# Two batches of a decode attention kernel taken pair by pair: one score loop, one pV loop, both softmaxes between them, the FFN first

## The chip, the cores and the metric

The kernel runs on one core of a Trainium2 chip. The metric is the device time of one execution in microseconds (us). Before the change it was 351.21 us, the median of five runs (350.96 to 351.4). The profiled executions have a span that is about 2 us shorter than the time of the run (349.2 us against 350.98), because the span starts and ends with the recorded instructions.

## The reference, cut to what matters

```python
# x: [2, 1, 512]   k_cache, v_cache: [2, 32, 4096, 128] bf16   wq: [512, 4096]   wo: [4096, 512]
q = (x @ wq)                       # 32 heads of 128, one query for each of 2 batches
p = softmax(q . k * 128 ** -0.5)   # over 4096 keys, for each head and batch
a = (p . v) @ wo
b = relu(x @ w1) @ w2              # FFN, 512 -> 1376 -> 512
g = sigmoid((x * gate_w).sum(-1))
return g * a + (1 - g) * b
```

K and V are 67 MB each, the weights 11 MB. All of it is read once: 145.43 MB.

## The kernel before

The heads are taken two at a time: a "pair" is two heads of one batch, 2 MB of K and 2 MB of V, and there are 32 pairs. One queue, that of SyncE, issues all large loads in one fixed order. Four buffers (`NSLOT`) hold pairs of K first and pairs of V afterwards. A load waits until the buffer's last user is done, so at most four pairs are in flight or in use:

```python
load("ld_wq", wq_sb[:, :, :], wq_in)
for n in range(64):                  # 0..31: K pairs, 32..63: V pairs
    waits = []
    if n >= NSLOT:
        prev = n - NSLOT             # the buffer is free after the last transpose of K pair prev,
        waits.append(f"T_{prev}_7" if prev < 32 else f"pv_{prev - 32}")   # or the last pV of V pair prev
    load(f"ld_kv_{n}", kv_sb[:, n % NSLOT, :, :], kv_in(n), waits=waits, sem=f"slot{n % NSLOT}")
    if n == 12:
        load("ld_w1", ...); load("ld_w2a", ...); load("ld_w2b", ...)
# ... then wo in five parts
```

For a K pair, TensorE transposes 64 blocks of 128x128 (`T`), VectorE and ScalarE copy them out of PSUM, and 16 matmuls make scores (`Sc`). For a V pair, 64 matmuls with two columns each accumulate pV (`PV`). TensorE's work is in loops of four pairs. Batch 0 has pairs 0 to 15, and its softmax runs while the scores of batch 1 are made. The softmax of batch 1 runs while pV of batch 0 is made:

```python
for g in range(2):                   # two score loops on TensorE
    P.begin_loop(NIT) ... T(g, p, ...), Sc(g, p) ... P.end_loop()
# ...
for i in range(32):
    evac(i)                          # copies out of PSUM (VectorE, ScalarE)
    if i == 17: row_max(0)           # softmax of batch 0, inside the K stage
    if i == 18: exps(0)
    if i == 19: denom_l(0)
ptrans(0)                            # transposes of the exponentials
denom(0)
# ...
for i in range(PER):
    stage_p(i)                       # exponentials of pair i, laid out for pV (VectorE)
    if i == 1:
        row_max(1); exps(1); denom_l(1)
for g in range(2):
    if g:
        ptrans(1); ...stage_p...; denom(1)
        ffn_h(); ffn_relu(); ffn_f() # FFN between the two pV loops
    P.begin_loop(NIT) ... PV(g, p) ... P.end_loop()
    ...
o_spread()
proj()                               # times wo, added to the FFN in PSUM
```

Of the kernel before, what the change touches and what calls it, by code (L numbers as in the profile page):

```python
# [14 lines left out]
PER = 4  # L15
NPAIR = 16
NIT = NPAIR // PER
NKT = 2
# [118 lines left out]
def bass_gated_mix__gqa_block_cached__dense_activation_relu__decode_kernel(  # L137
# [49 lines left out]
    oA = sb("oA", [128, 2, 32, 4], b16)  # L187
    os_sb = sb("os_sb", [128, 32, 2], b16)
    out_sb = sb("out_sb", [98, 128], b16)

# [39 lines left out]
    def kv_in(n):  # L230
        c = A_k_cache if n < 32 else A_v_cache
        b, hp = divmod(n % 32, 16)
        return c[b, 2 * hp:2 * hp + 2].rearrange("h (p r) d -> (h p) r d", p=64)
# [6 lines left out]
    load("ld_gw", gw_sb[:, :], gw_in, eng="act")  # L240
    load("ld_wq", wq_sb[:, :, :], wq_in)
    for n in range(64):
        waits = []
        if n >= NSLOT:
            prev = n - NSLOT
            waits.append(f"T_{prev}_7" if prev < 32 else f"pv_{prev - 32}")
        load(f"ld_kv_{n}", kv_sb[:, n % NSLOT, :, :], kv_in(n), waits=waits, sem=f"slot{n % NSLOT}")
        if n == 12:
            load("ld_w1", w1_sb[:, :, :], w1_in)
            load("ld_w2a", w2_sb[:, 0:10, :], w2a_in)  # L250
            load("ld_w2b", w2_sb[0:96, 10, :], w2b_in)
    WO_CUTS = (0, 16, 24, 28, 30, 32)
# [60 lines left out]

    def T(g, p, qs):
        for q in qs:
            for rr in range(8):
                r = 8 * q + rr

                def waits(t, q=q):
                    i = NPAIR * g + PER * t + p  # L320
                    w = [f"ld_kv_{i}"] if q == 0 else []
                    if q >= 4:
                        w.append(f"ev_{i}_{q - 4}")
                    elif p:
                        w.append(f"ev_{i - 1}_{q + 4}")
                    return w + (["qm_0", "qm_1", "g"] if g == 0 and p == 0 and q == 0 else [])

                P.add("pe", lambda e, iv, q=q, rr=rr, r=r: e.transpose(bank16(4 + q % 4, rr * 128, 128), kv_sb[:, p, r, :], ident16[:, :]),  # L328
                      waits=waits if rr == 0 else [],
                      signal=(lambda t, q=q: f"T_{NPAIR * g + PER * t + p}_{q}") if rr == 7 else None)  # L330

    def Sc(g, p):
        for c in range(8):
            for hh in range(2):
                def waits(t, c=c):
                    i = NPAIR * g + PER * t + p
                    return ([f"qst_{i}"] if c == 0 else []) + ([f"ev_{i}_{c}"] if c >= 4 else [])

                P.add("pe", lambda e, iv, c=c, hh=hh: e.matmul(  # L339
                    S_chunk(g, c), lhsT=qst[:, p, hh, :], rhs=kt_sb[:, p % NKT, 8 * c:8 * c + 8, 64 * hh:64 * hh + 64],  # L340
                    start=False, stop=True, tile_position=(0, 32 * (c % 4)), skip_group_check=True),
                    waits=waits if hh == 0 else [],
                    signal=(lambda t: f"sc_{NPAIR * g + PER * t + p}") if (c, hh) == (7, 1) else None)

# [12 lines left out]
    def stage_q(i):  # L357
        p = i % PER
        P.add("pool", lambda e: e.tensor_copy(out=qst[:, p, :, :], in_=qmask[:, 2 * i:2 * i + 2, :]),  # L359
              waits=[f"qm_{i // NPAIR}"] + ([f"sc_{i - PER}"] if i >= PER else []), signal=f"qst_{i}", sem=f"qs{p}")  # L360

    for g in range(2):
        P.begin_loop(NIT)
        T(g, 0, range(8))
        for p in range(PER):
            if p + 1 < PER:
                T(g, p + 1, range(2))
            Sc(g, p)
            if p + 1 < PER:
                T(g, p + 1, range(2, 8))  # L370
        P.end_loop()


    def row_max(g):
        P.add("dve", lambda e: e.tensor_reduce(out=m4[:, g:g + 1], in_=S_region(g), axis=AX.X, op=ALU.max),  # L375
              waits=[f"sc_{NPAIR * g + NPAIR - 1}"], signal=f"m4_{g}")
        for q in range(4):
# [38 lines left out]
    def stage_p(i):  # L416
        g, hp = divmod(i, NPAIR)
        p = i % PER
        for hh in range(2):
            base = PSB[0:64, 2048 * g:2048 * g + 2048].rearrange("p (b k j) -> p b k j", b=2, k=32)  # L420
            P.add("dve", lambda e, hh=hh, base=base: e.tensor_copy(  # L421
                out=pst[64 * hh:64 * hh + 64, p, :, hh].rearrange("p (b k) -> p b k", b=2), in_=base[:, :, :, 2 * hp + hh]),
                waits=[f"pt_{g}_2", f"pt_{g}_3", "c_ps"] + ([f"pv_{i - PER}"] if i >= PER else []),
                signal=f"pst_{i}" if hh else None, sem=f"ps{p}")

    def o_norm(i):
        g, hp = divmod(i, NPAIR)
        P.add("dve", lambda e: e.tensor_tensor(out=oT[:, g, 2 * hp:2 * hp + 2], in0=o_col(i % PER), in1=rg[:, g, 2 * hp:2 * hp + 2],  # L428
                                               op=ALU.mult),
              waits=[f"pv_{i}", f"rg_{g}"], signal=f"oT_{i}", sem=f"on{i % PER}")  # L430

    def PV(g, p):
        for r in range(64):
            b, blk = p_place(r)

            def waits(t):
                i = NPAIR * g + PER * t + p
                return [f"ld_kv_{32 + i}", f"pst_{i}"] + ([f"oT_{i - 2}"] if i >= 2 else [])
            P.add("pe", lambda e, iv, r=r, k=32 * b + blk: e.matmul(o_col(p), lhsT=kv_sb[:, p, r, :], rhs=pst[:, p, k, :],  # L439
                                                                    start=(r == 0), stop=(r == 63)),  # L440
                  waits=waits if r == 0 else [], signal=(lambda t: f"pv_{NPAIR * g + PER * t + p}") if r == 63 else None)


    def ffn_h():
        for ft in range(11):
            n = 128 if ft < 10 else 96
            for t in range(4):
                P.add("pe", lambda e, ft=ft, t=t, n=n: e.matmul(  # L448
                    bank(MISC, 64 + 2 * ft, 2, 0, n), lhsT=w1_sb[:, t, ft:1280:10] if ft < 10 else w1_sb[:, t, 1280:1376],
                    rhs=xT_sb[:, t, :], start=(t == 0), stop=(t == 3)),  # L450
                    waits=["ld_w1", "rg_1"] if ft + t == 0 else [], signal="hT" if (ft, t) == (10, 3) else None)

    def ffn_relu():
        P.add("act", lambda e: e.activation(out=hr_sb[:, 0:20], in_=bank(MISC, 64, 20), func=ACT.Relu), waits=["hT"])  # L454
        P.add("act", lambda e: e.activation(out=hr_sb[0:96, 20:22], in_=bank(MISC, 84, 2, 0, 96), func=ACT.Relu), signal="hr")
        for n, lo, hi in ((128, 0, 10), (96, 10, 11)):
# [4 lines left out]

    def ffn_f():
        for ft in range(11):
            n = 128 if ft < 10 else 96
            for c in range(4):
                P.add("pe", lambda e, ft=ft, n=n, c=c: e.matmul(
                    acc(c), lhsT=hT_sb[0:n, ft, :], rhs=w2_sb[0:n, ft, 128 * c:128 * c + 128], start=False, stop=True,
                    tile_position=(0, 32 * c), skip_group_check=True),
                    waits=["hTs", "ld_w2a", "ld_w2b"] if ft + c == 0 else [])

# [13 lines left out]
    def proj():  # L484
        for r in range(32):
            for c in range(4):
                w = (["os_sb"] if r == 0 else []) + ([f"ld_wo_{WO_CUTS.index(r)}"] if r in WO_CUTS else [])
                P.add("pe", lambda e, r=r, c=c: e.matmul(acc(c), lhsT=os_sb[:, r, :], rhs=wo_sb[:, r, 128 * c:128 * c + 128],  # L488
                                                         start=False, stop=True, tile_position=(0, 32 * c), skip_group_check=True),
                      waits=w if c == 0 else [], signal="proj" if (r, c) == (31, 3) else None)  # L490

    for i in range(32):
        stage_q(i)
    for i in range(32):
        evac(i)
        if i == 17:
            row_max(0)
        if i == 18:
            exps(0)
        if i == 19:  # L500
            denom_l(0)
    ptrans(0)
    denom(0)
    P.add("pe", lambda e: e.matmul(bank(ACC, 0, 128), lhsT=zt[:, 0:128], rhs=zt[:, 0:128], start=True, stop=True))
    for i in range(PER):
        stage_p(i)
        if i == 1:
            row_max(1)
            exps(1)
            denom_l(1)  # L510
    for g in range(2):
        if g:
            ptrans(1)
            for i in range(PER):
                stage_p(NPAIR + i)
            denom(1)
            ffn_h()
            ffn_relu()
            ffn_f()
        P.begin_loop(NIT)  # L520
        for p in range(PER):
            PV(g, p)
        P.end_loop()
        for i in range(NPAIR * g, NPAIR * g + NPAIR):
            o_norm(i)
            if i + PER < NPAIR * (g + 1):
                stage_p(i + PER)
    o_spread()
    proj()
    P.add("dve", lambda e: e.tensor_copy(out=out_sb[:, :], in_=bank(ACC, 0, 128, 0, 98)), waits=["proj"], signal="res")  # L530
    for b, eng in enumerate(("sp", "act")):
# [53 lines left out]
```

## Time and profile before

| | value | where it is read |
|---|---|---|
| time | 351.21 us | median of five runs |
| bytes read, share of the 16 DMA engines | 145.43 MB, 98.3% | table of DMA queues |
| a 2 MB pair on the wire | 4.89 us | step between landings |
| TensorE for a K pair, unhindered | 4.80 us | timeline |
| TensorE for a V pair | 1.86 us | timeline |
| last score to first pV | 3.3 us | chain of waits |
| instruction fetches (queue q8; e8, with longer TensorE code, has 22 where e2 has 10) | 13 of 16 KB | table of DMA queues |

These lines of the page of the kernel before are the busy shares of the span in 40 slices (each digit a tenth) and the DMA queues. A queue's columns are packets, MB, and the share of sixteen engines' time.

```profile
span 349.2 us, 11060 instructions
...
PE   2489999995699899999998643343266643443244
...
PEclk9999999999599999999999555555555555555555
DMA  8999999999999999999999999999999999999994
GB/s 331 419 426 428 428 430 423 430 423 411 428 425 428 423 428 430 424 432 428 428 426 430 423 424 432 424 428 432 428 426 432 418 426 430 430 430 426 426 420 158
...
q1 hardware_dynamic: 10488, 145.43, 98.3%
q8 instruction: 13, 0.21, 0.3%
```

The DMA row is 9 from the second slice to the last but one. TensorE is also at 9 in the K stage, but only because it works at the pace of the loads (4.80 us of work a pair, and a pair lands every 4.89 us), and in the V stage (from slice 23 on) it waits most of the time (1.86 us of work in 4.89). The kernel is bound by the bytes: the loads take 98.3% of the sixteen engines' time. No change to an engine's work can save time here unless it also changes what the DMA queue does (e4 fills a hole in TensorE's work and stays at 350.96 us against 351.04).

The chain of waits of the kernel before, at the boundary between the K and the V stage (start us, duration us, what; L339 makes scores, L400 transposes the exponentials, L409 sums denominators, L439 is pV):

```profile
185.89 1.54 PE PS L339 x16
187.43 1.82 PE PS L400 x64
189.25 0.35 PE PS L409 x2
...
190.77 3.19 PE PS L439 x116
193.96 3.07 issue
```

From the last score at 187.43 to the first pV at 190.77 there are 3.3 us. Pair 0 is finished at about 192.5, estimated from the 3.19 us of 116 matmuls, and then the load of V pair 4 is requested.

The stages of 2 us of the same kernel around that time (window, PE busy (count), PEld, DVE, ACT, POOL, granted TensorE clock, DMA share, GB/s):

```profile
194.00:196.00 2.00, 0.00 (x0) 0.00 (x0) 0.82 (x5) 1.09 (x2) 0.00 (x0) 0.50 1.02 414
196.00:198.00 2.00, 0.96 (x36) 0.97 (x37) 1.17 (x7) 0.00 (x0) 0.00 (x0) 0.50 0.98 418
198.00:200.00 2.00, 2.00 (x81) 2.00 (x79) 0.62 (x4) 0.00 (x0) 0.00 (x0) 0.50 1.04 442
200.00:202.00 2.00, 0.58 (x22) 0.50 (x19) 0.00 (x0) 0.00 (x0) 0.00 (x0) 0.50 0.99 410
```

The DMA share stays at 1: V pair 4 was requested before V pair 3 had come in.

One more reading is needed. Each load of a pair leaves sixteen landing records in the trace, read here as one for each of the sixteen DMA engines. The table gives the first and the last of the sixteen landings, in us from the start of the span.

```
kernel before        first engine   last engine   spread
K pair 0                 17.26          17.89       0.63
K pair 1                 22.14          23.86       1.72
V pair 3                195.82         197.90       2.08
V pair 4                200.72         202.79       2.07
last part of wo         342.84         346.07       3.24
```

At K pair 1, fifteen engines landed between 22.14 and 22.74 and one at 23.86. An instruction fetch had started at 17.6 us. The lateness stays in the landing records of this trace, and more engines are late after further fetches: one engine over 1.4 us behind the first at K pair 1, three at K pair 4 (fetches had started at 27.8 and 34.3), nine at the last part of wo. The time ends with the last engine: the last matmuls start at 346.12, when it has landed at 346.07. The first engine was finished 3.24 us before it.

### The profile page before, as it was taken

To read this page: it belongs to the slowest core of one execution; us is meant where nothing else is said; L and a number is where in the kernel's file an instruction comes from. 1 tells how busy PE (TensorE), PEld (TensorE's weight loads), DVE (VectorE), ACT (ScalarE), POOL (GpSimd) and SP (SyncE) were. 2 spreads that over 40 slices of the span, in tenths; PEclk is the share of its full clock that TensorE was granted. 3 is DMA by queue.
4 is the path that set the end of the run, shared out by engine and by line. 5 is a ranking of instruction groups with operands and counts; after the bars stand their busy time and mean duration, and the time that the engine had idled before them with its cause. 6 is when DMAs were issued, how large, how long until landed. Compare 5 with 4: busy or idle time off the path is not lost.

```text
span 349.2 us, 11060 instructions
## 1 busy us (share of the span) xinstructions
PE 239.4 (69%) x5115; PEld 205.1 (59%) x5115; DVE 132.4 (38%) x293; ACT 99.4 (28%) x105; POOL 12.0 (3%) x52
## 2 busy tenths in 40 slices
PE   2489999995699899999998643343266643443244
PEld 0478787884588678888787642343266643443233
DVE  0147566764167867667675411110003111110010
ACT  1045654763165577666562100000000000000000
POOL 5000000000000000000000000000000000000000
PEclk9999999999599999999999555555555555555555
DMA  8999999999999999999999999999999999999994
GB/s 331 419 426 428 428 430 423 430 423 411 428 425 428 423 428 430 424 432 428 428 426 430 423 424 432 424 428 432 428 426 432 418 426 430 430 430 426 426 420 158
DMA packets 10520, 145.69 MB, mean 417 GB/s; under 512 B 1187, under 2 KB 1286, under 8 KB 1670
## 3 DMA queue, kind: packets, MB, share of 16 engines
q1 hardware_dynamic: 10488, 145.43, 98.3%
q8 instruction: 13, 0.21, 0.3%
q14 instruction: 5, 0.04, 0.0%
q10 hardware_dynamic: 14, 0.00, 0.0%
HBM read 145.43 MB, written 0.00 MB: 416 GB/s over the span
## 4 chain that ended last, share of the span: by engine, by line
DMA 49%; PE 44%; issue 3%; DVE 2%; ACT 1%; SPq 1%; DVEq 0%
DMA kv_sb<-in_A_v_cache_dram 29%; PE PS L328 29%; DMA kv_sb<-in_A_k_cache_dram 13%; PE PS L339 9%; DMA wo_sb<-in_A_wo_dram 7%; PE PS L439 5%; SPq L237 1%; DVE kt_sb L355 1%; ACT kt_sb L352 1%; PE PS L400 1%; ACT L388 0%; ACT E L388 0%; DVE m L375 0%; DVE mq L378 0%; DVE negM L383 0%
## 5 line engine op out<-in xcount | busy, mean ns | idle before, releaser
L328 PEld LDWEIGHTS PS<-ident,kv_sb 128*128 128x128 bf16 x2048 | 117.8, 99 | 26.4 <-issue 22.8
L328 PE MATMUL PS<-ident,kv_sb 128*128 128x128 bf16 x2048 | 124.8, 222 | 11.1 <-DMA kv_sb<-in_A_k_cache_dram 9.0
L355 DVE COPY kt_sb<-PS 128x1024 bf16<-128x1024 bf16 x160 | 105.6, 688 | 61.4 <-PE PS L328 61.2
L352 ACT ACTIVATE kt_sb<-PS 128x1024 bf16<-128x1024 bf16 x96 | 94.2, 1023 | 79.8 <-PE PS L328 79.8
L439 PE MATMUL PS<-pst,kv_sb 128*128 128x2 bf16 x2048 | 59.1, 165 | 78.9 <-DMA kv_sb<-in_A_v_cache_dram 69.7
L439 PEld LDWEIGHTS PS<-pst,kv_sb 128*128 128x128 bf16 x2048 | 57.1, 104 | 81.2 <-issue 67.5
L428 DVE TENSOR_TENSOR oT<-PS,rg 128x2 bf16<-128x2 f32 x32 | 5.1, 160 | 118.7 <-PE PS L439 118.7
L339 PE MATMUL PS<-kt_sb,qst 128*32 128x512 bf16 x512 | 39.1, 390 | 0.0
L454 ACT ACTIVATE hr_sb<-PS 128x20 f32<-128x20 f32 x1 | 0.2, 188 | 73.1 <-PE PS L448 73.1
L339 PEld LDWEIGHTS PS<-kt_sb,qst 128*32 128x32 bf16 x512 | 13.4, 96 | 12.9 <-DVE kt_sb L355 3.6
L421 DVE COPY pst<-PS 64x64 bf16<-64x64 bf16 x64 | 14.3, 224 | 3.6 <-PE PS L400 2.8
L359 POOL COPY qst<-qmask 128x64 bf16<-128x64 bf16 x32 | 7.4, 238 | 155.0 <-PE PS L339 140.1
L488 PE MATMUL PS<-wo_sb,os_sb 128*2 128x128 bf16 x128 | 4.3, 305 | 3.2 <-DMA wo_sb<-in_A_wo_dram 3.1
L304 PE MATMUL PS<-xT_sb,wq_sb 128*128 128x2 bf16 x128 | 3.6, 165 | 3.5 <-DMA wq_sb<-in_A_wq_dram 3.5
L304 PEld LDWEIGHTS PS<-xT_sb,wq_sb 128*128 128x128 bf16 x128 | 3.5, 104 | 3.6 <-DMA wq_sb<-in_A_wq_dram 3.6
L488 PEld LDWEIGHTS PS<-wo_sb,os_sb 128*2 128x2 bf16 x128 | 2.9, 112 | 4.4 <-DMA wo_sb<-in_A_wo_dram 2.2
L400 PEld LDWEIGHTS PS<-ident,E 32*64 32x64 bf16 x128 | 4.7, 129 | 0.4 <-issue 0.4
L400 PE MATMUL PS<-ident,E 32*64 32x32 bf16 x128 | 4.9, 195 | 0.0
L388 ACT ACTIVATE E<-PS,negM 128x1024 bf16<-128x1024 f32 x2 | 2.2, 1114 | 7.8 <-DVE negM L383 7.8
L448 PE MATMUL PS<-xT_sb,w_sb 128*128 128x2 bf16 (+1 forms) x44 | 2.8, 199 | 2.2 <-DVE rg L412 2.2
L448 PEld LDWEIGHTS PS<-xT_sb,w_sb 128*128 128x128 bf16 (+1 forms) x44 | 2.7, 161 | 2.3 <-issue 2.3
L288 PE MATMUL PS<-ident,gw_sb 1*128 1x1 bf16 x4 | 0.3, 172 | 4.8 <-DMA gw_sb<-in_gate_w_dram 4.8
(50 smaller groups left out, 26.5 us busy)
## 6 DMA issues: line engine op xcount, KB each, us to landing
kv_sb<-in_A_k_cache_dram SPq DMA_DIRECT2D x32, 2048.0 KB, 14.2
kv_sb<-in_A_v_cache_dram SPq DMA_DIRECT2D x32, 2048.0 KB, 17.6
wq_sb<-in_A_wq_dram SPq DMA_DIRECT2D x1, 4096.0 KB, 12.2
wo_sb<-in_A_wo_dram SPq DMA_DIRECT2D x1, 2048.0 KB, 22.1
w_sb<-in_B_w_dram SPq DMA_DIRECT2D x1, 1376.0 KB, 17.1
w_sb<-in_B_w_dram SPq DMA_DIRECT2D x1, 1280.0 KB, 20.1
wo_sb<-in_A_wo_dram SPq DMA_DIRECT2D x1, 1024.0 KB, 24.1
wo_sb<-in_A_wo_dram SPq DMA_DIRECT2D x1, 512.0 KB, 24.9
```

Source lines behind the costliest of these rows:

```text
L304: P.add("pe", lambda e, h=h, t=t: e.matmul(bank(7, 2 * h, 2), lhsT=wq_sb[:, t, h * 128:(h + 1) * 128], rhs=xT_sb[:, t, :], start=(t == 0), ...
L328: P.add("pe", lambda e, iv, q=q, rr=rr, r=r: e.transpose(bank16(4 + q % 4, rr * 128, 128), kv_sb[:, p, r, :], ident16[:, :]), waits=waits ...
L339: P.add("pe", lambda e, iv, c=c, hh=hh: e.matmul(S_chunk(g, c), lhsT=qst[:, p, hh, :], rhs=kt_sb[:, p % NKT, 8 * c:8 * c + 8, 64 * hh:64 * ...
L352: P.add("act", lambda e, dst=dst, src=src: e.activation(out=dst, in_=src, func=ACT.Copy), waits=w, signal=f"ev_{i}_{q}", sem=f"ev{p}{q}")
L355: P.add("dve", lambda e, dst=dst, src=src: e.tensor_copy(out=dst, in_=src), waits=w, signal=f"ev_{i}_{q}", sem=f"ev{p}{q}")
L359: P.add("pool", lambda e: e.tensor_copy(out=qst[:, p, :, :], in_=qmask[:, 2 * i:2 * i + 2, :]), waits=[f"qm_{i // NPAIR}"] + ([f"sc_{i - P ...
L400: P.add("pe", lambda e, q=q, b=b, blk=blk, src=src: e.transpose(bank16(2 * g + b, 32 * blk, 32, 0, 64), src, ident16[32 * q:32 * q + 32, 3 ...
L421: P.add("dve", lambda e, hh=hh, base=base: e.tensor_copy(out=pst[64 * hh:64 * hh + 64, p, :, hh].rearrange("p (b k) -> p b k", b=2), in_=b ...
L428: P.add("dve", lambda e: e.tensor_tensor(out=oT[:, g, 2 * hp:2 * hp + 2], in0=o_col(i % PER), in1=rg[:, g, 2 * hp:2 * hp + 2], op=ALU.mult ...
L439: P.add("pe", lambda e, iv, r=r, k=32 * b + blk: e.matmul(o_col(p), lhsT=kv_sb[:, p, r, :], rhs=pst[:, p, k, :], start=(r == 0), stop=(r = ...
L448: P.add("pe", lambda e, ft=ft, t=t, n=n: e.matmul(bank(MISC, 64 + 2 * ft, 2, 0, n), lhsT=w1_sb[:, t, ft:1280:10] if ft < 10 else w1_sb[:, ...
L488: P.add("pe", lambda e, r=r, c=c: e.matmul(acc(c), lhsT=os_sb[:, r, :], rhs=wo_sb[:, r, 128 * c:128 * c + 128], start=False, stop=True, ti ...
```

## The change

The intent was a simpler program: pair i is heads pair i // 2 of batch i % 2, so that there is one score loop and one pV loop of eight rounds each. Both softmaxes come between the loops. The FFN's weights are loaded first, the FFN is computed before the scores, and its result waits in SBUF to be added in the final copy.

```diff
-NPAIR = 16
-NIT = NPAIR // PER
+NIT = 32 // PER
...
-        b, hp = divmod(n % 32, 16)
+        hp, b = divmod(n % 32, 2)
...
     load("ld_wq", wq_sb[:, :, :], wq_in)
+    load("ld_w1", ...); load("ld_w2a", ...); load("ld_w2b", ...)      # moved up from after K pair 12
...
+    ffn_h()
+    ffn_relu()
+    ffn_f()                  # ends with a copy to f_sb
+    scores()                 # one loop
...
     for i in range(32):
         evac(i)
-        if i == 17:
-            row_max(0)
-        if i == 18:
-            exps(0)
-        if i == 19:
-            denom_l(0)
-    ptrans(0)
-    denom(0)
...
+    for g in range(2):
+        row_max(g)
+        exps(g)
+        ptrans(g)
+    for i in (0, 2, 1, 3):
         stage_p(i)
...
     for g in range(2):
-        if g: ... ptrans(1), stage_p, denom(1), FFN ...
-        P.begin_loop(NIT)
-        for p in range(PER):
-            PV(g, p)
-        P.end_loop()
+        denom_l(g)
+        denom(g)
+    P.begin_loop(NIT)
+    for p in range(PER):
+        PV(p)
+    P.end_loop()
...
-    tensor_copy(out=out_sb, in_=bank(ACC, ...))
+    tensor_tensor(out=out_sb, in0=bank(ACC, ...), in1=f_sb, op=ALU.add)
```

More of the change, by code (lines that the diff above doesn't have):

```diff
@@ L188, in bass_gated_mix__gqa_block_cached__dense_activation_relu__decode_kernel @@
     os_sb = sb("os_sb", [128, 32, 2], b16)
+    f_sb = sb("f_sb", [98, 128], f32)
     out_sb = sb("out_sb", [98, 128], b16)
@@ L241, in bass_gated_mix__gqa_block_cached__dense_activation_relu__decode_kernel @@
     load("ld_wq", wq_sb[:, :, :], wq_in)
+    load("ld_w1", w1_sb[:, :, :], w1_in)
+    load("ld_w2a", w2_sb[:, 0:10, :], w2a_in)
+    load("ld_w2b", w2_sb[0:96, 10, :], w2b_in)
     for n in range(64):
@@ L247, in bass_gated_mix__gqa_block_cached__dense_activation_relu__decode_kernel @@
         load(f"ld_kv_{n}", kv_sb[:, n % NSLOT, :, :], kv_in(n), waits=waits, sem=f"slot{n % NSLOT}")
-        if n == 12:
-            load("ld_w1", w1_sb[:, :, :], w1_in)
-            load("ld_w2a", w2_sb[:, 0:10, :], w2a_in)
-            load("ld_w2b", w2_sb[0:96, 10, :], w2b_in)
     WO_CUTS = (0, 16, 24, 28, 30, 32)
@@ L311, in bass_gated_mix__gqa_block_cached__dense_activation_relu__decode_kernel, with T @@
         P.add("dve", fn, waits=["qT", "c_qm"], signal=f"qm_{g}")
-    def T(g, p, qs):
+    def T(p, qs):
         for q in qs:
@@ L319, in waits @@
                 def waits(t, q=q):
-                    i = NPAIR * g + PER * t + p
+                    i = PER * t + p
                     w = [f"ld_kv_{i}"] if q == 0 else []
@@ L325, in waits, with Sc @@
                         w.append(f"ev_{i - 1}_{q + 4}")
-                    return w + (["qm_0", "qm_1", "g"] if g == 0 and p == 0 and q == 0 else [])
+                    return w + (["qm_0", "qm_1", "f_sb"] if p == 0 and q == 0 else [])
                 P.add("pe", lambda e, iv, q=q, rr=rr, r=r: e.transpose(bank16(4 + q % 4, rr * 128, 128), kv_sb[:, p, r, :], ident16[:, :]),
                       waits=waits if rr == 0 else [],
-                      signal=(lambda t, q=q: f"T_{NPAIR * g + PER * t + p}_{q}") if rr == 7 else None)
-    def Sc(g, p):
+                      signal=(lambda t, q=q: f"T_{PER * t + p}_{q}") if rr == 7 else None)
+    def Sc(p):
         for c in range(8):
@@ L335, in waits @@
                 def waits(t, c=c):
-                    i = NPAIR * g + PER * t + p
+                    i = PER * t + p
                     return ([f"qst_{i}"] if c == 0 else []) + ([f"ev_{i}_{c}"] if c >= 4 else [])
                 P.add("pe", lambda e, iv, c=c, hh=hh: e.matmul(
-                    S_chunk(g, c), lhsT=qst[:, p, hh, :], rhs=kt_sb[:, p % NKT, 8 * c:8 * c + 8, 64 * hh:64 * hh + 64],
+                    S_chunk(p % 2, c), lhsT=qst[:, p, hh, :], rhs=kt_sb[:, p % NKT, 8 * c:8 * c + 8, 64 * hh:64 * hh + 64],
                     start=False, stop=True, tile_position=(0, 32 * (c % 4)), skip_group_check=True),
                     waits=waits if hh == 0 else [],
-                    signal=(lambda t: f"sc_{NPAIR * g + PER * t + p}") if (c, hh) == (7, 1) else None)
+                    signal=(lambda t: f"sc_{PER * t + p}") if (c, hh) == (7, 1) else None)
     def evac(i):
@@ L358, in stage_q, with scores @@
         p = i % PER
-        P.add("pool", lambda e: e.tensor_copy(out=qst[:, p, :, :], in_=qmask[:, 2 * i:2 * i + 2, :]),
-              waits=[f"qm_{i // NPAIR}"] + ([f"sc_{i - PER}"] if i >= PER else []), signal=f"qst_{i}", sem=f"qs{p}")
-    for g in range(2):
+        P.add("pool", lambda e: e.tensor_copy(out=qst[:, p, :, :], in_=qmask[:, 32 * (i % 2) + i // 2 * 2:32 * (i % 2) + i // 2 * 2 + 2, :]),
+              waits=[f"qm_{i % 2}"] + ([f"sc_{i - PER}"] if i >= PER else []), signal=f"qst_{i}", sem=f"qs{p}")
+    def scores():
         P.begin_loop(NIT)
-        T(g, 0, range(8))
+        T(0, range(8))
         for p in range(PER):
             if p + 1 < PER:
-                T(g, p + 1, range(2))
-            Sc(g, p)
+                T(p + 1, range(2))
+            Sc(p)
             if p + 1 < PER:
-                T(g, p + 1, range(2, 8))
+                T(p + 1, range(2, 8))
         P.end_loop()
@@ L375, in row_max @@
         P.add("dve", lambda e: e.tensor_reduce(out=m4[:, g:g + 1], in_=S_region(g), axis=AX.X, op=ALU.max),
-              waits=[f"sc_{NPAIR * g + NPAIR - 1}"], signal=f"m4_{g}")
+              waits=[f"sc_{30 + g}"], signal=f"m4_{g}")
         for q in range(4):
@@ L416, in stage_p @@
     def stage_p(i):
-        g, hp = divmod(i, NPAIR)
+        hp, g = divmod(i, 2)
         p = i % PER
@@ L426, in o_norm @@
     def o_norm(i):
-        g, hp = divmod(i, NPAIR)
+        hp, g = divmod(i, 2)
         P.add("dve", lambda e: e.tensor_tensor(out=oT[:, g, 2 * hp:2 * hp + 2], in0=o_col(i % PER), in1=rg[:, g, 2 * hp:2 * hp + 2],
@@ L430, in o_norm, with PV @@
               waits=[f"pv_{i}", f"rg_{g}"], signal=f"oT_{i}", sem=f"on{i % PER}")
-    def PV(g, p):
+    def PV(p):
         for r in range(64):
@@ L436, in waits @@
             def waits(t):
-                i = NPAIR * g + PER * t + p
+                i = PER * t + p
                 return [f"ld_kv_{32 + i}", f"pst_{i}"] + ([f"oT_{i - 2}"] if i >= 2 else [])
@@ L440, in PV @@
                                                                     start=(r == 0), stop=(r == 63)),
-                  waits=waits if r == 0 else [], signal=(lambda t: f"pv_{NPAIR * g + PER * t + p}") if r == 63 else None)
+                  waits=waits if r == 0 else [], signal=(lambda t: f"pv_{PER * t + p}") if r == 63 else None)
     def ffn_h():
@@ L448, in ffn_h @@
                 P.add("pe", lambda e, ft=ft, t=t, n=n: e.matmul(
-                    bank(MISC, 64 + 2 * ft, 2, 0, n), lhsT=w1_sb[:, t, ft:1280:10] if ft < 10 else w1_sb[:, t, 1280:1376],
+                    bank(5, 2 * ft, 2, 0, n), lhsT=w1_sb[:, t, ft:1280:10] if ft < 10 else w1_sb[:, t, 1280:1376],
                     rhs=xT_sb[:, t, :], start=(t == 0), stop=(t == 3)),
-                    waits=["ld_w1", "rg_1"] if ft + t == 0 else [], signal="hT" if (ft, t) == (10, 3) else None)
+                    waits=["ld_w1", "gwb"] if ft + t == 0 else [], signal="hT" if (ft, t) == (10, 3) else None)
     def ffn_relu():
-        P.add("act", lambda e: e.activation(out=hr_sb[:, 0:20], in_=bank(MISC, 64, 20), func=ACT.Relu), waits=["hT"])
-        P.add("act", lambda e: e.activation(out=hr_sb[0:96, 20:22], in_=bank(MISC, 84, 2, 0, 96), func=ACT.Relu), signal="hr")
+        P.add("act", lambda e: e.activation(out=hr_sb[:, 0:20], in_=bank(5, 0, 20), func=ACT.Relu), waits=["hT"])
+        P.add("act", lambda e: e.activation(out=hr_sb[0:96, 20:22], in_=bank(5, 20, 2, 0, 96), func=ACT.Relu), signal="hr")
         for n, lo, hi in ((128, 0, 10), (96, 10, 11)):
@@ L462, in ffn_f @@
     def ffn_f():
+        P.add("pe", lambda e: e.matmul(bank(4, 0, 128), lhsT=zt[:, 0:128], rhs=zt[:, 0:128], start=True, stop=True), waits=["hTs"])
         for ft in range(11):
@@ L466, in ffn_f @@
                 P.add("pe", lambda e, ft=ft, n=n, c=c: e.matmul(
-                    acc(c), lhsT=hT_sb[0:n, ft, :], rhs=w2_sb[0:n, ft, 128 * c:128 * c + 128], start=False, stop=True,
+                    bank(4, 0, 128, 32 * c, 32 * c + 2), lhsT=hT_sb[0:n, ft, :], rhs=w2_sb[0:n, ft, 128 * c:128 * c + 128], start=False, stop=True,
                     tile_position=(0, 32 * c), skip_group_check=True),
-                    waits=["hTs", "ld_w2a", "ld_w2b"] if ft + c == 0 else [])
+                    waits=["ld_w2a", "ld_w2b"] if ft + c == 0 else [], signal="f" if (ft, c) == (10, 3) else None)
+        P.add("dve", lambda e: e.tensor_copy(out=f_sb[:, :], in_=bank(4, 0, 128, 0, 98)), waits=["f"], signal="f_sb")
     def o_spread():
@@ L488, in proj @@
                 P.add("pe", lambda e, r=r, c=c: e.matmul(acc(c), lhsT=os_sb[:, r, :], rhs=wo_sb[:, r, 128 * c:128 * c + 128],
-                                                         start=False, stop=True, tile_position=(0, 32 * c), skip_group_check=True),
+                                                         start=(r == 0), stop=(r == 31), tile_position=(0, 32 * c), skip_group_check=True),
                       waits=w if c == 0 else [], signal="proj" if (r, c) == (31, 3) else None)
+    ffn_h()
+    ffn_relu()
+    ffn_f()
+    scores()
     for i in range(32):
@@ L495, in bass_gated_mix__gqa_block_cached__dense_activation_relu__decode_kernel @@
         evac(i)
-        if i == 17:
-            row_max(0)
-        if i == 18:
-            exps(0)
-        if i == 19:
-            denom_l(0)
-    ptrans(0)
-    denom(0)
-    P.add("pe", lambda e: e.matmul(bank(ACC, 0, 128), lhsT=zt[:, 0:128], rhs=zt[:, 0:128], start=True, stop=True))
-    for i in range(PER):
+    for g in range(2):
[3 more added lines that the diff above has]
+    for i in (0, 2, 1, 3):
         stage_p(i)
-        if i == 1:
-            row_max(1)
-            exps(1)
-            denom_l(1)
     for g in range(2):
-        if g:
-            ptrans(1)
-            for i in range(PER):
-                stage_p(NPAIR + i)
-            denom(1)
-            ffn_h()
-            ffn_relu()
-            ffn_f()
-        P.begin_loop(NIT)
-        for p in range(PER):
-            PV(g, p)
-        P.end_loop()
-        for i in range(NPAIR * g, NPAIR * g + NPAIR):
-            o_norm(i)
-            if i + PER < NPAIR * (g + 1):
-                stage_p(i + PER)
+        denom_l(g)
[4 more added lines that the diff above has]
+    P.end_loop()
+    for i in range(32):
+        o_norm(i)
+        if i + PER < 32:
+            stage_p(i + PER)
     o_spread()
     proj()
-    P.add("dve", lambda e: e.tensor_copy(out=out_sb[:, :], in_=bank(ACC, 0, 128, 0, 98)), waits=["proj"], signal="res")
+    P.add("dve", lambda e: e.tensor_tensor(out=out_sb[:, :], in0=bank(ACC, 0, 128, 0, 98), in1=f_sb[:, :], op=ALU.add),
+          waits=["proj"], signal="res")
     for b, eng in enumerate(("sp", "act")):
```

## The prediction

> **What bounds the kernel now.** The DMA. In the stage table (5 us windows) the DMA share is 0.98 to 1.05 from 5 to 340 us; the queue table gives 145.43 MB, 98.3% of 16 engines. The chain of waits names TensorE (44%) too, but TensorE only keeps pace: 4.80 us a K pair against 4.89 us for its 2 MB, and per V pair 1.86 us against 4.89. So what is removed from an engine saves nothing by itself; the change matters where it starves the queue or alters what the queue carries.
>
> **What the change moves.**
> 1. w1/w2 (2.8 MB, 6.5 us) go ahead of K0: same bytes; K0 lands near 24.4 us instead of 17.9, and TensorE's idle stretch of 85 to 90 us, with the half clock after it, goes. The FFN hides before K0. Worth 0.
> 2. The first softmax, now hidden in the K stage, and the second, hidden behind pV, both move to the boundary. Now TensorE goes from the last score (187.4) to the first pV (190.8) in 3.4 us. After, from durations in the timeline: row max with small copies 2.7 us, exponential 1.2, second row max 2.7 (overlapping the first exponential), second exponential 1.2, transposes 1.9 warm or 3.0 at half clock, stage copies 0.95, two denominators about 1.3: some 11 us.
> 3. K31 lands at about 178 as before; last transpose 183; last score 184.5, three us earlier than now; first pV starts at 195 to 196 and ends at 197 to 198.5. Only then is V4's load issued; its data starts 1 to 1.5 us later: 198.5 to 200. The fast DMA engines finish V3 at 195.8, the slow ones at about 197.5. So the queue, never dry before, is dry for 2 to 4 us on the fast engines, about 1 to 2.5 on the slow ones. Later pVs outrun the loads, so it happens once.
> 4. Removed: TensorE's program shrinks (two loops instead of four). The queue table shows 13 instruction fetches of 16 KB; the landing records show each delaying one of the sixteen engines by about 1.1 us for good; at the end the engines are 3.2 us apart (342.8 to 346.1). I expect 7 to 9 fetches, none hitting an engine twice, and the dry moment lets the engines realign: 1 to 1.5 us back. [...]
> 5. The final add replaces a copy of the same shape (0.29 us): 0.
>
> **Sum.** V4's first data at 199.2, then 147.0 us of bytes (a fast engine takes that now, 195.8 to 342.8), 1.8 us spread of engines, 3.1 us tail, 2 us outside the span: 353.1. Point 353.0, range 350.4 to 356.0. Faster by over 2%: 0.01; within 2%: 0.94; slower: 0.05.
>
> **Right or wrong.** Right if: GB/s stays 425 to 430 except one dip of 2 to 4 us at 195 to 200; bytes unchanged; instruction fetches drop to 7 to 9 and the last landings spread by 2 us or less; no half clock near 90 us; TensorE needs about 11 us between last score and first pV. With no dip step 3 is wrong, and the time about 350.
>
> **What would make it wrong.** An instruction fetch stalling the transposes or the first pV (such stalls are 2.5 to 3.1 us in the V stage now), added to the dry time: 356. TensorE staying at half clock in the K stage: much slower. Interleaving batches lowering the rate of reads: 1% of rate is 3.4 us.

The sum: 199.2 + 147.0 + 1.8 + 3.1 + 2 = 353.1.

## The result, and the profile after

The changed kernel takes 354.64 us (median of five runs, 354.42 to 354.64) against 351.21 us. The ratio is 1.0097, with a 95% interval of 1.0082 to 1.0112. A ratio here is the mean time of one kernel's runs over the mean of the other's in the same rounds, so it is not quite the ratio of the medians. The change costs about 3.4 us.

The same lines of the page, after:

```profile
span 352.9 us, 11059 instructions
...
PE   2539999999999999999986824433344333443244
...
PEclk9999999999999999999996555555555555555555
DMA  8999999999999999999999599999999999999994
GB/s 342 400 417 431 423 425 427 430 425 433 426 423 431 428 431 427 431 427 423 431 427 424 204 438 423 438 420 436 425 431 426 425 433 423 435 423 427 431 420 160
...
q1 hardware_dynamic: 10488, 145.43, 97.4%
q8 instruction: 8, 0.13, 0.1%
```

There is one hole in the DMA row, the 5 in the slice of 194 to 203 us, where 204 GB/s moved instead of about 427. Everything else goes at the old rate, with the old bytes. The half clock near 90 us (0.50 at 90 to 95 us before, 1.00 now) is gone, and TensorE's row has no 5 and 6 there any more, yet this saves nothing.

The chain of waits after the change, at the boundary (L374 is the row maximum, L387 the exponential, L399 transposes the exponentials, L408 sums denominators, L438 is pV):

```profile
183.72 1.14 DVE m L374
...
186.36 1.21 ACT E L387 x2
...
187.62 5.77 PE PS L399 x128
...
194.69 0.65 PE PS L408 x2
...
196.20 0.63 PE PS L408 x2
196.83 6.82 PE PS L438 x256
203.65 0.02 issue
203.67 18.58 DMA kv_sb<-in_A_v_cache_dram
```

The last score ended at 184.4, 3.0 us earlier than before. But the timeline has the first pV starting at 196.6, a boundary of 12.3 us instead of 3.3. Pair 0 was finished at about 198.5 and V pair 4 was requested at 198.55, while V pair 3 had come in at 195.6 (first engine) to 197.9 (last).

The stages of 2 us around it:

```profile
194.00:196.00 2.00, 0.63 (x2) 0.50 (x2) 1.19 (x6) 0.00 (x0) 0.00 (x0) 0.50 0.73 311
196.00:198.00 2.00, 1.80 (x52) 1.80 (x53) 0.74 (x3) 0.00 (x0) 0.00 (x0) 0.50 0.16 66
198.00:200.00 2.00, 2.00 (x81) 2.00 (x79) 0.53 (x3) 0.00 (x0) 0.00 (x0) 0.50 0.48 98
200.00:202.00 2.00, 2.00 (x81) 2.00 (x79) 0.57 (x4) 0.00 (x0) 0.00 (x0) 0.50 0.76 279
202.00:204.00 2.00, 1.64 (x62) 1.55 (x59) 0.81 (x6) 0.00 (x0) 0.00 (x0) 0.50 0.99 418
```

The DMA share falls to 0.16. The queue restarts at 199.5 (first packet). These stages count a packet where it starts, so the 98 GB/s of 198 to 200 are 1.5 us of nothing and twelve packets in the last 0.5 us. The slow restart is seen in the packets themselves: the twenty packets of 16 KB that started from 199.5 to 200.7 took 1.16 us in the mean, where 0.61 is usual, and only after about 201.2 do they take 0.61 again.

```
kernel after         first engine   15th engine   last engine   spread
V pair 3                195.62         197.44        197.87       2.25
V pair 4                205.33         206.12        207.56       2.23
last part of wo         347.49         348.77        349.75       2.27
```

A step between two loads is 4.89 us when nothing is missing. From V pair 3 to V pair 4 the first engine needed 9.70, so 4.8 us were lost on it. Yet the last landing of the program came only 3.7 us later than before (349.75 against 346.07), because the spread at the end fell from 3.24 to 2.27 us: there are 8 instruction fetches instead of 13, and after the dry stretch fifteen engines landed within 0.8 us of each other again, instead of 1.8. The sixteenth stayed 1.4 us behind. A fetch started at 203.9, in the middle of the first load after the restart, which fits, but the records do not say which engine served it.

### The profile page after: what moved, and what is told of

It reads as the page before. It is cut to its first block, busy times and chain, and to the rows that moved or that the text cites. A ratio compares the mean times of both kernels' runs of the same rounds, so it can differ in the third digit from the quotient of the medians.

```text
span 352.9 us, 11059 instructions
## 1 busy us (share of the span) xinstructions
PE 238.4 (68%) x5115; PEld 204.8 (58%) x5115; DVE 132.4 (38%) x294; ACT 99.5 (28%) x105; POOL 12.0 (3%) x52
## 4 chain that ended last, share of the span: by engine, by line
PE 51%; DMA 44%; DVE 2%; SPq 1%; issue 1%; ACT 0%; DVEq 0%
PE PS L327 34%; DMA kv_sb<-in_A_v_cache_dram 30%; PE PS L338 10%; DMA wo_sb<-in_A_wo_dram 7%; DMA kv_sb<-in_A_k_cache_dram 7%; PE PS L438 5%; PE PS L399 2%; SPq L237 1%; DVE kt_sb L354 0%; PE PS L408 0%; ACT E L387 0%; DVE m L374 0%; DVE negM L382 0%; DVE pst L420 0%; DVE mq L377 0%
## 5 line engine op out<-in xcount | busy, mean ns | idle before, releaser
L327 PEld LDWEIGHTS PS<-ident,kv_sb 128*128 128x128 bf16 x2048 | 116.5, 99 | 19.2 <-issue 14.8
L438 PE MATMUL PS<-pst,kv_sb 128*128 128x2 bf16 x2048 | 58.8, 165 | 86.3 <-DMA kv_sb<-in_A_v_cache_dram 86.3
L438 PEld LDWEIGHTS PS<-pst,kv_sb 128*128 128x128 bf16 x2048 | 57.1, 104 | 88.1 <-issue 65.7
L338 PE MATMUL PS<-kt_sb,qst 128*32 128x512 bf16 x512 | 38.3, 382 | 0.0
L399 PE MATMUL PS<-ident,E 32*64 32x32 bf16 x128 | 5.8, 210 | 3.2 <-ACT E L387 3.2
L399 PEld LDWEIGHTS PS<-ident,E 32*64 32x64 bf16 x128 | 5.7, 150 | 3.7 <-ACT E L387 3.7
L387 ACT ACTIVATE E<-PS,negM 128x1024 bf16<-128x1024 f32 x2 | 2.2, 1113 | 3.6 <-DVE negM L382 3.6
```

What stands on the lines that cost most here:

```text
L327: P.add("pe", lambda e, iv, q=q, rr=rr, r=r: e.transpose(bank16(4 + q % 4, rr * 128, 128), kv_sb[:, p, r, :], ident16[:, :]), waits=waits ...
L338: P.add("pe", lambda e, iv, c=c, hh=hh: e.matmul(S_chunk(p % 2, c), lhsT=qst[:, p, hh, :], rhs=kt_sb[:, p % NKT, 8 * c:8 * c + 8, 64 * hh: ...
L399: P.add("pe", lambda e, q=q, b=b, blk=blk, src=src: e.transpose(bank16(2 * g + b, 32 * blk, 32, 0, 64), src, ident16[32 * q:32 * q + 32, 3 ...
L438: P.add("pe", lambda e, iv, r=r, k=32 * b + blk: e.matmul(o_col(p), lhsT=kv_sb[:, p, r, :], rhs=pst[:, p, k, :], start=(r == 0), stop=(r = ...
```

## The experiments

Each ran in the same rounds and on the same chip as the kernel before: one chip for e1 to e4, another for e5 to e9. That kernel took 351.04 us (e1 to e4) and 351.06 us (e5 to e8, and e9). The theory: the kernel is bound by the queue, and the longer boundary lets it run dry, since a fifth V pair is requested only when the first pV is done. The rivals: interleaved reads are slower in memory; the FFN first delays the K stage; whatever is moved to the boundary costs its own length.

| run | median us | ratio to before (95%) | first pV starts, us | step of first engine, V3 to V4, us |
|---|---|---|---|---|
| before | 351.21 | | 190.8 | 4.90 |
| after | 354.64 | 1.0097 (1.0082 to 1.0112) | 196.6 | 9.70 |
| e1 | 352.03 | 1.0021 (1.0005 to 1.0038) | 194.6 | 7.63 |
| e2 | 350.88 | 0.9994 (0.9978 to 1.0011) | 196.8 | 4.89 |
| e3 | 354.53 | 1.0100 (1.0083 to 1.0117) | 196.9 | 9.82 |
| e4 | 350.96 | 0.9999 (0.9982 to 1.0015) | 188.6 | 4.88 |
| e5 | 351.07 | 1.0003 (0.9986 to 1.0020) | 191.9 | 4.95 |
| e6 | 353.77 | 1.0074 (1.0057 to 1.0090) | 196.1 | 9.32 |
| e7 | 351.15 | 1.0000 (0.9983 to 1.0016) | 193.4 | 6.72 |
| e8 | 353.18 | 1.0062 (1.0046 to 1.0079) | 196.9 | 4.90 |
| e9 | 350.66 | 0.9991 (0.9977 to 1.0004) | 194.5 | 4.89 |

In e2, e8 and e9, which have six buffers, the load that can come late is V pair 6. The step of the first engine from V5 to V6 was 5.63, 5.79 and 4.91 us there.

### e1: the denominators out of the boundary's chain

```diff
     for g in range(2):
         row_max(g)
         exps(g)
-        ptrans(g)
-    for i in (0, 2, 1, 3):
-        stage_p(i)
-    for g in range(2):
-        denom_l(g)
-        denom(g)
+    for g in range(2):
+        denom_l(g)
+    for g in range(2):
+        ptrans(g)
+        stage_p(g)
+        stage_p(g + 2)
+        denom(g)
```

> The changed kernel with the two denominators taken out of the boundary's chain (done while the exponentials and transposes run). Theory (the queue runs dry because pV of pair 0 ends too late): first pV starts 2.6 us sooner, near 194.0 instead of 196.6, the dry stretch of the DMA falls from 4.8 us to about 2.2 us on the fast engines, and the time falls from 354.6 to about 352.1. Rival (the loss is elsewhere: order of reads, FFN first): no change, 354.6.

The timeline of e1 has the first pV at 194.6 (start us, duration us, engine, line, operation):

```profile
194.63 6.99 PE L438 MATMUL PS<-pst,kv_sb 128*128 128x2 bf16 x256
```

It started 2.0 us sooner (2.6 expected), the lost time on the first engine fell from 4.8 to 2.7 us, and the time fell by 2.6 us to 352.03. An edit of a few lines, which removes no work at all, takes back most of the loss. The rivals that put the loss elsewhere cannot explain this.

### e2: two more V buffers, the boundary as long as it is

The memory of wq, 4 MB, is not read after 16.6 us. The first two V pairs go there. Their pV is written out ahead of the loop, the loop has seven rounds for pairs 2 to 29, and pairs 30 and 31 follow it.

```diff
+        if n in (32, 33):
+            load(f"ld_kv_{n}", wq_sb[...half n - 32...], kv_in(n), waits=["qT"], ...)
+            continue
+        m = n if n < 32 else n - 2          # place of the load in the ring of four
...
+    PV1(0); PV1(1)
-    P.begin_loop(NIT)
+    P.begin_loop(NIT - 1)
...
+    PV1(30); PV1(31)
```

> The changed kernel with two more V buffers (the first two V pairs go to the memory of wq, which nobody reads after the projection), boundary left as long as it is. Theory (dry queue): two loads, 9.8 us, more are in flight at the boundary, so no dry slice at all, and the time is 349.8 to 351.5, at or below the kernel before. Rival (the softmax at the boundary costs by itself, or the reads are slower): 354 or more.

The stages of 5 us of e2:

```profile
195.00:200.00 5.00, 4.13 (x123) 4.00 (x124) 1.87 (x8) 0.00 (x0) 0.00 (x0) 0.50 0.99 423
200.00:205.00 5.00, 3.01 (x114) 2.95 (x112) 1.06 (x6) 0.00 (x0) 0.00 (x0) 0.50 1.01 423
205.00:210.00 5.00, 4.22 (x158) 4.14 (x156) 1.06 (x6) 0.00 (x0) 0.00 (x0) 0.50 1.00 397
```

The boundary is as long as in the changed kernel, with the first pV at 196.8, and the loss is gone: 350.88 us, level with the kernel before. A small part of the expectation failed: I had expected no dry moment at all, but pV of the third pair stalled 2.0 us, and the first engines waited 0.7 us before the load of V pair 6. The last engine did not wait (its step was 4.91 us). So the softmax at the boundary costs nothing by itself. It costs what it exceeds the loads in flight by.

### e3: the old order of reads

```diff
-        hp, b = divmod(n % 32, 2)
+        b, hp = divmod(n % 32, 16)
```

> The changed kernel reading K and V in the order of the kernel before (all of one batch, then the other); wrong result on purpose. Theory: the order of addresses is without effect, 354.6 within 0.3. Rival (interleaved reads are slower in memory): 351 to 352.

354.53 us against 354.64 (ratios 1.0100 and 1.0097): the order of addresses has no effect that these runs can tell. (The kernel pairs K and V with the wrong heads. The comparison with the reference is too coarse to see this exchange.)

### e4: only the FFN part of the change

The kernel before, with the weights loaded before K, `ffn_h`, `ffn_relu` and `ffn_f` ahead of the score loops, and the FFN added in the final copy, as in the diff of the change. The batches still come one after the other.

> The kernel before with only the FFN part of the change: its weights loaded before K, FFN before the scores, added in the final copy; batches one after the other as before. Theory: worth nothing, 351.2 within 0.7; no TensorE gap at 85 to 90 us and no half clock there. Rival (FFN first costs, as K starts 8 us later): 353 to 355.

The stage of 85 to 90 us, first in the kernel before and then in e4:

```profile
85.00:90.00 5.00, 0.01 (x1) 0.04 (x2) 0.00 (x0) 0.00 (x0) 0.00 (x0) 0.58 1.01 429
```

```profile
85.00:90.00 5.00, 5.00 (x80) 4.02 (x79) 3.14 (x6) 2.61 (x4) 0.24 (x1) 1.00 0.99 423
```

TensorE was idle in this stage and is now fully busy, at full clock instead of 0.58. The DMA share is 1.01 and 0.99, the same within the noise of these stages. The time is 350.96 against 351.04. A visible hole in an engine that does not bound this kernel was worth nothing.

### e5: only the first softmax moved to the boundary

```diff
     for i in range(32):
         evac(i)
-        if i == 17:
-            row_max(0)
-        if i == 18:
-            exps(0)
-        if i == 19:
-            denom_l(0)
+    row_max(0)
+    exps(0)
+    denom_l(0)
     ptrans(0)
```

> The kernel before with only its first softmax held back to the boundary (two score loops, two pV loops and the FFN in the middle stay). Theory (a boundary costs only what exceeds the loads in flight): TensorE takes about 7.5 us from last score to first pV instead of 3.4, but ends its scores 2 to 3 us sooner, so pair 0 ends by about 194, before the fast engines finish V3 at 195.6: no or almost no dry stretch, 351.2 within 0.7. Rival (each microsecond moved to the boundary costs a microsecond): 354 to 355.

The last score and the first pV in the timeline of e5:

```profile
183.16 1.61 PE L339 MATMUL PS<-kt_sb,qst 128*32 128x512 bf16 x16
...
191.85 3.25 PE L439 MATMUL PS<-pst,kv_sb 128*128 128x2 bf16 x116 [1.07 <-DVE pst L421]
```

351.07 us against 351.06. The last score ended at 184.8 and pV began at 191.9, so the boundary doubled from 3.3 to 7.1 us for nothing. This is the run that refutes "each microsecond moved there costs one". It does not show slack of 3.8 us, though: the scores ended 2.6 us sooner than in the kernel before, so pV began only 1.1 us later, and V pair 4 was requested at 193.7, which is 2.1 us before the first landing of V pair 3 (195.8). With that the slack was about used up, since the next load came 0.4 us late on the first engine (a step of 5.26 us, after an instruction fetch). In the changed kernel the request came 2.9 us after that landing.

### e6 and e7: holding TensorE's clock over the boundary

```diff
+    for _ in range(14):
+        P.add("pe", lambda e: e.matmul(bank(ACC, 0, 512), lhsT=zt[:, 0:128], rhs=zt[:, :], start=True, stop=True))
     for g in range(2):
         row_max(g)
```

e6 is the changed kernel with this edit, e7 is e1 with it.

> The changed kernel with 14 idle matmuls of zeros (0.22 us each) between the last score and the transposes, while TensorE waits for the row maxima anyway, to hold its clock. Theory: the transposes took 2.7 and 3.0 us because the granted clock fell to 0.5 at 187 us; held at 1.0 they take 1.9 each, first pV starts about 1.8 us sooner, time near 352.8. If the clock falls all the same, or the matmuls delay the transposes: 354.6 or more.

> Both remedies of the boundary: denominators early and the idle matmuls. Theory: pair 0 ends near 194.6, V4's data starts near 196.5, dry below 1 us on the fast engines and none on the slow ones; time 350.2 to 351.2, level with the kernel before or just below. If the two do not add: 352.

The two sets of transposes in the timeline of e6:

```profile
187.74 1.89 PE L399 MATMUL PS<-ident,E 32*64 32x32 bf16 x64
...
190.47 2.32 PE L399 MATMUL PS<-ident,E 32*64 32x32 bf16 x64 [0.84 <-ACT E L387]
```

The first set took 1.89 us, as expected, but the second cannot start before the second exponential is done at 190.4, and it started at nearly the same time as in the changed kernel. The clock fell at 191.6 in the middle of it. First pV came 0.6 us sooner, not 1.8, and the time was 353.77, not 352.8. My expectation had added up the durations and forgotten the wait between them. In e7 the first pV came at 193.4 and the time was 351.15, inside what was expected, though the first engine still lost 1.8 us and not less than 1. That the time was level all the same is in part luck: the last engine ended 2.2 us after the first, where the kernel before has 3.24.

Taken together, after, e6, e1 and e7 form a series. From the first to the last the first pV comes 3.2 us sooner (196.6 to 193.4) and the time falls by 3.5 us (354.64 to 351.15).

One relation explains the misses of e2 and e7. In the seven runs that lost over half a microsecond (after, e1, e2, e3, e6, e7, e8), the loss on the first engine is the time from its last landing before the gap to the request of the late load, plus 1.8 to 2.2 us. In e7 the request came at 195.56, just as V pair 3 first landed (195.60), and 1.8 us were lost. In e2 it came 1.2 us before the landing (204.25 and 205.41), and 0.7 us were lost. So in these runs a request had to come about 2 us before the first engine ran out. In after, e1, e3, e6 and e7 about 1.0 us of this is the time from the request to the first packet.

### e8: what an instruction fetch costs the loads

e2 with its pV loop written out in a straight line:

```diff
-    P.begin_loop(NIT - 1)
-    for p in range(PER):
-        PV(p)
-    P.end_loop()
-    PV1(30)
-    PV1(31)
+    for i in range(2, 32):
+        PV1(i)
```

> The kernel with two more V buffers, its pV loop written out in a straight line: the same work, some 12 more instruction fetches of 16 KB during the V stage, each of which stalls TensorE (which has 3 us a pair to spare) and, by theory, takes one of the sixteen DMA engines 1.1 us. Theory: 12 x 1.1 / 16 = 0.8 us on the mean engine, 0.8 to 2.2 on the last: 351.7 to 353.1 against 350.9. Rival (fetches are free for the loads): 350.9.

The queue of instruction fetches of e8 has 22 packets where e2 has 10:

```profile
q8 instruction: 22, 0.36, 0.4%
```

```
last part of wo      first engine   8th engine   last engine   spread
e2, 10 fetches          343.48         344.15       346.00       2.52
e8, 22 fetches          343.59         345.92       347.94       4.35
```

The time rose by 2.3 us to 353.18, just above the top of what I had expected (353.1). The first engine ended at nearly the same time (343.59 and 343.48), so the queue was not starved more than in e2. The eighth and the last ended 1.8 and 1.9 us later. The same kernel with the same bytes is slower because its code is longer. (e2 and e8 ran on different chips, and the kernel before took 351.04 and 351.06 us beside them.)

### e9: more buffers and early denominators together

> Two more V buffers and early denominators together: the version that should suit the interleaved order best. First pV near 194.6 and V6 requested 2 us sooner than with the buffers alone, where the fast engines alone waited 0.7 us (V7 to V8) and the last engine none. Theory (the last of the sixteen engines sets the end): nothing more to win, 350.9 within 0.4, level with the kernel before. If the fast engines' wait counted: 350.2.

350.66 us, ratio 0.9991 (0.9977 to 1.0004): level with the kernel before, as expected. The first engines no longer waited, and this won nothing that these runs can tell from zero. No version beat the kernel before clearly. What remains is the bytes.

## Why the prediction was right or wrong

The time, 354.64, is inside the range of 350.4 to 356.0 and 1.6 us above the point of 353.0. The mechanism was right, and sizes were off in points 2 to 4.

1. **The FFN first is worth 0.** Right: e4 gives 350.96 against 351.04.
2. **A boundary of some 11 us.** It was 12.3. The denominators took 2.2 us instead of 1.3 (194.4 to 196.6), and both sets of transposes, 5.8 us one after the other, ran at half clock (0.50 from 187.2 on). So the first pV came at 196.6, past the 195 to 196 of the prediction.
3. **The queue runs dry.** Right in place and nearly in time: pair 0 ended at 198.5, the late edge of the range, and the first packet of V pair 4 came at 199.5 against 199.2 in the sum. From the landing of V pair 3 to that packet the queue was dry for 3.9 us on the first engine and 2.1 on the fifteenth, inside the 2 to 4 and 1 to 2.5 that I had said. What was mis-sized is the restart. I let the queue run at full rate from its first packet. But its first packets took up to 1.63 us instead of 0.61, and the first engine landed V pair 4 5.8 us after the first packet instead of 4.9: 0.9 us more. So the first engine lost 4.8 us in all, and the fifteenth 3.8.
4. **Fewer fetches, engines realign.** 8 fetches, as forecast (7 to 9). Fifteen engines did line up, but one stayed 1.4 us late, and the spread at the end was 2.27 us where the sum had 1.8 and the list of signs "2 us or less".
5. **The final add costs 0.** Right: 0.29 us in both.

Estimated from these terms, 353.1 + 0.3 (first packet) + 0.9 (restart) + 0.5 (spread) - 0.2 (1.8 us outside the span, not 2) is 354.6. Of the three risks named, none came about: no fetch stalled the first pV (it ran without a gap from 196.6), the clock did not stay low in the K stage (1.00 from 30.2 to 187.2), and e3 excludes the order of reads (354.53 us).

The fetches here are 16,384 bytes each. e8 has 24 pairs of 128 instructions more written out than e2, and 12 more fetches: 256 instructions a fetch, an estimate from these two runs.

In the clock records of the two traces, the stretches between two changes of the granted clock last 64.85, 10.24 and 95.57 us in the kernel before, and 157.01 us in the changed kernel. They are 19, 3, 28 and 46 times 3.413 us, so the changes seem to keep to a step of that length, an estimate from these four stretches. The granted clock fell at 187.2 here, 2.8 us after the last score, which is less than one such step, and 2.0 us after it in e8.

## What to carry to other kernels

In a kernel whose DMA queue is always full, price a change by one question: when is the next load requested, and has the queue anything left at that moment? Work moved into the gap was free as long as the next load was requested some 2 us before the first DMA engine ran out (e5), and cost about its full length beyond that (the changed kernel, e6, e1, e7). So compare the moment of that request with the loads in flight, and either shorten its chain (e1) or lend it dead memory as more buffers (e2). The end was set by the slowest of the sixteen DMA engines, so long straight-line code cost time although the engine that runs it waited most of the V stage (e8: 12 more fetches, the last engine 1.9 us later, the run 2.3 us longer).

## What else the traces show of fetches, the restart and the clock

- Under the full DMA queue of these runs the fetches were not hidden. TensorE stalled 3.07 and 2.47 us in the V stage of the kernel before (from 193.96 and 200.58), next to fetches that started at 194.5 and 200.5. 12 more fetches (e8 against e2) made the last DMA engine 1.9 us later and the run 2.3 us longer; e8 is the one with the pV loop written out.
- One engine was 1.1 us behind the other fifteen right after the first fetch (K pair 1 of the kernel before), and the spread grew to 3.24 us in that run of 13 fetches. In the changed kernel it was 1.8 us over fifteen engines before the queue ran dry, and 0.8 us after.
- A pV loop of 512 matmul and weight-load instructions, worth two fetches by the estimate of 256, ran seven more rounds in the changed kernel without a fetch (none between 203.9 and 347.8 us).
- On the dry queue of the changed kernel, the first packet came 1.0 us after the request (198.55 to 199.53), and the packets of the next 1.2 us took 1.16 us in the mean instead of 0.61.
- In the changed kernel transposes of 128x128 blocks alone were running when the clock rose: from 26.2 us on they start 107 ns apart, from 30.2 us on 56 ns apart, and the first score comes only at 32.6. (The PEclk row shows 9 there from the start, because the records of the clock begin only at 30.2.) In e6 the transposes of 32x64 blocks did not hold the clock: it fell at 191.6, 4.0 us after the last full-width matmul, though they had run from 187.7 to 189.6 and again from 190.5 on. In the changed kernel 256 pV matmuls back to back (7.0 us) did not raise it from 0.50.
